# Attention scores without a mask product, zeros written into the exponentials by GpSimd, and low parts moved from GpSimd to VectorE

## The chip, the cores and the metric

One core of a Trainium2 chip runs the whole program. The metric is the device time of one execution in microseconds (us); for the kernel before it is the median of three runs. TensorE is called PE below, VectorE DVE, ScalarE ACT, GpSimd POOL, and the queue that issues the transfers SP.

## The reference

Twelve heads in each of two batches go through causal attention over 448 positions, and two feed-forward layers follow on the 896 tokens.

```python
scores = (q @ k.T) / 8
scores = where(mask, -1e9, scores)          # mask: key later than query
scores = scores - max(scores)
attn = exp(scores); attn = attn / (sum(attn) + 1e-9)
x = attn @ v                                # heads side by side: 896 x 768
h = x @ w_in                                # 768 x 1024
solu = h * softmax(h)
ln = (solu - mean) / sqrt(var + 1e-6) * g_ln
y = ln @ w_out                              # 1024 x 768
out = relu(y @ w_in2) ** 2 @ w_out2         # 768 x 2048 x 768
```

## The kernel before

The matrix products run on numbers split in two: a high part (a cast to the format that PE multiplies fast) and a low part (what the cast left out), in three products, high by high, high by low and low by high. So every operand costs one cast on ACT and one subtraction on DVE or POOL. The weights come in eight-byte form and are first put together as fp32 on DVE, by one tensor_scalar and two scalar_tensor_tensor (L150, L151, L152: "wf").

**Attention** goes over 12 pairs of heads, i = 0 to 11, two heads on the two halves of the partitions. For a pair: `load_r` and `load_v` bring k, q and v; `H` casts k and q (ACT), `L` makes their low parts (the tile LO, L272). `S0a`, `S0b`, `S0c` are products of the high parts alone (tile mxp), and `mxa`, `mxb`, `mxc` take from them, on DVE, the largest unmasked score of each query (L298, with a mask tile MK added). `mT` turns these maxima into a row on PE, `row` copies it (ACT), and `rowd` sends it to one partition of the tile MR by DMA (L323). `Sa` and `Sb` are the scores of the two halves of a pair's work, transposed (keys on the partitions): three products of parts, then one of MR with a constant of minus ones (NEG1), which subtracts the maxima, and then a masking product (L353) of a table TR of 0 and -1e30 with a shifted identity ID. Half a covers the first block of 128 keys for all queries, and the fourth block for the last 64; half b covers the second and the third block. `ea1` and `eb1` are the exponentials (ACT, into one of the buffers PP), `Ua` and `Ub` multiply by v, and a column of ones beside v gives the sums. `EA`, `EB` copy the result out, `sums`, `recips`, `rcd`, `spread` send the sums through DVE and a DRAM tile and back to 64 partitions (tile bc) by three DMAs, `norm` multiplies on POOL (tile x, one buffer, L419), and `x_hi`, `x_lo` split it. Pair 0 gets its maxima into the scores in another way (L359).

**The first layer** (`h0` to `h6`, seven tiles of 128 tokens, six chunks c of W1) begins while the last pairs run, the second (`y0`, `y1`) follows, then the two products with 2048 columns. W1 is loaded (`lq`, `ld`), expanded (`wf`), cast (`wh`, ACT) and its low part is made (`wl`: chunks 1, 3 and 5 on POOL, the others on DVE). `fl` are products whose result nobody reads, at the start.

What sets the order of all this is a list written into the kernel, SEQ: each name is an operation and its number a pair, a chunk or a tile. Each engine runs its own part of the list in that order, and waits where an operand or a buffer isn't ready. The products mxp, mT and U share four PSUM banks.

Of the kernel before, what the change touches and what calls it, by code (L numbers as in the profile page):

```python
# [29 lines left out]
load_r.2 fl.7 mxb.0 fl.8 lq.5 L.1 fl.9 S0c.1 fl.10 mxc.1 mxr.0 fl.11 S0a.1 S0b.1 Sa.0 mxb.1 H.2 load_r.3 lq.0 mxa.1  # L30
lq.6 L.2 mT.1 S0a.2 row.1 Sb.0 ea1.0 mxa.2 load_r.4 rowd.1 S0b.2 eb1.0 Ua.0 mxb.2 lq.1 lq.8 H.3 S0c.2 L.3 Ub.0 mxc.2
load_r.5 mT.2 Sa.1 row.2 EA.0 rowd.2 EB.0 load_v.2 S0a.3 ea1.1 S0b.3 sums.0 mxa.3 Sb.1 lq.9 lq.2 mxb.3 S0c.3 Sa.2 H.4
mxc.3 eb1.1 L.4 S0c.4 mT.3 ea1.2 mxc.4 Sb.2 recips.0 row.3 lq.3 S0b.4 eb1.2 rcd.0 Ua.1 mxb.4 load_v.3 rowd.3 S0a.4
Ub.1 mxa.4 spread.0 wf.0 load_r.6 Ua.2 lq.7 EA.1 H.5 mT.4 Sa.3 row.4 EB.1 norm.0 sums.1 S0b.5 load_v.4 ea1.3 Ub.2
mxb.5 rowd.4 L.5 load_r.7 x_hi.0 recips.1 Sb.3 EA.2 rcd.1 EB.2 S0c.5 sums.2 S0a.5 H.6 mxc.5 Sa.4 mxa.5 eb1.3 L.6 S0a.6
spread.1 mT.5 Sb.4 recips.2 lq.10 row.5 mxa.6 ea1.4 rcd.2 rowd.5 S0b.6 x_lo.0 H.7 Ua.3 mxb.6 load_r.8 norm.1 S0c.6
Ub.3 mxc.6 L.7 x_hi.1 spread.2 S0b.7 Sa.5 eb1.4 mxb.7 EA.3 EB.3 S0c.7 mT.6 mxc.7 Sb.5 wh.0 sums.3 x_lo.1 row.6 wl.0
ea1.5 S0a.7 rowd.6 Ua.4 H.8 load_v.5 norm.2 recips.3 load_r.9 mxa.7 eb1.5 rcd.3 Ub.4 lq.11 wf.1 mT.7 EA.4 Sa.6
load_v.6 EB.4 row.7 sums.4 S0c.8 ea1.6 Sb.6 spread.3 rowd.7 L.8 mxc.8 S0b.8 H.9 Ua.5 mxb.8 load_v.7 x_hi.2 eb1.6
x_lo.2 Ub.5 recips.4 wh.1 norm.3 rcd.4 load_r.10 S0a.8 Sa.7 mxa.8 L.9 EA.5 spread.4 x_hi.3 mT.8 S0a.9 EB.5 Sb.7 mxa.9  # L40
row.8 sums.5 ea1.7 load_r.11 x_lo.3 S0c.9 Ua.6 H.10 rowd.8 mxc.9 norm.4 eb1.7 load_v.8 recips.5 S0b.9 rcd.5 Ub.6 mxb.9
ld.5 wl.1 x_hi.4 mT.9 EA.6 Sa.8 row.9 EB.6 x_lo.4 sums.6 S0a.10 ea1.8 Sb.8 spread.5 L.10 mxa.10 load_v.9 rowd.9 S0b.10
H.11 Ua.7 mxb.10 ld.3 norm.5 S0c.10 Ub.7 mxc.10 recips.6 rcd.6 wf.2 mT.10 EA.7 Sa.9 row.10 eb1.8 S0b.11 EB.7 Sb.9
x_hi.5 spread.6 ea1.9 sums.7 L.11 mxb.11 Ua.8 load_v.10 rowd.10 x_lo.5 S0a.11 Ub.8 mxa.11 norm.6 recips.7 rcd.7 S0c.11
Sa.10 mxc.11 ld.4 wf.3 EA.8 eb1.9 mT.11 Ua.9 row.11 ea1.10 rowd.11 Sb.10 x_hi.6 spread.7 wh.3 Ub.9 wh.2 eb1.10 wl.2
Sa.11 EB.8 x_lo.6 sums.8 load_v.11 Sb.11 norm.7 ea1.11 h0.0 recips.8 wf.4 rcd.8 EA.9 Ua.10 eb1.11 x_hi.7 EB.9 h0.1
spread.8 sums.9 x_lo.7 wh.4 h1.0 wl.3 Ua.11 recips.9 norm.8 rcd.9 Ub.10 wf.5 h1.1 x_hi.8 spread.9 h0.2 h1.2 wl.4 wh.5
h0.3 EA.10 x_lo.8 EB.10 wl.5 h1.3 sums.10 h0.4 norm.9 recips.10 Ub.11 rcd.10 h1.4 EA.11 x_hi.9 spread.10 EB.11 x_lo.9
h0.5 sums.11 h1.5 mx.0 h2.0 norm.10 ex.0 recips.11 mx.1 rcd.11 load_g.0 h2.1 mu.0 x_hi.10 h2.2 spread.11 x_lo.10 sq.0
de.0 h2.3 ex.1 va.0 pw.0 h2.4 mu.1 norm.11 h2.5 h3.0 mx.2 x_hi.11 h3.1 fa.0 de.1 ln.0 x_lo.11 h3.2 lw.0 ex.2 h3.3 sq.1  # L50
de.2 mu.2 h4.0 va.1 sq.2 h3.4 va.2 lw.1 of.0 T.0 pw.2 pw.1 h3.5 Th.0 h4.1 fa.2 mx.3 h4.2 fa.1 ex.3 Tl.0 lw.2 h4.3 ln.2
of.1 h5.0 oh.0 ln.1 h4.4 ol.0 de.3 h4.5 mu.3 lw.3 h5.1 of.2 sq.3 T.1 oh.1 h5.2 Th.1 mx.4 h5.3 Tl.1 ex.4 lw.4 h5.4 va.3
ol.1 pw.3 h5.5 fa.3 mu.4 ln.3 h6.0 of.3 sq.4 T.2 lw.5 T.3 Th.2 mx.5 h6.1 Tl.2 ex.5 h6.2 oh.2 mu.5 h6.3 Th.3 de.4 h6.4
lw.6 oh.3 Tl.3 sq.5 h6.5 va.4 ol.2 pw.4 y0.0 mx.6 de.5 ex.6 ol.3 lw.7 fa.4 l2.2 y0.1 de.6 ln.4 mu.6 l2.1 l2.0 of.4
y0.2 va.5 oh.4 of.5 pw.5 y0.3 ol.4 fa.5 of.6 ln.5 y0.4 oh.5 sq.6 ol.5 va.6 of.7 T.4 pw.6 y0.5 Th.4 oh.6 Tl.4 oh.7 ol.6
T.5 fa.6 y0.6 Th.5 ln.6 Tl.5 ol.7 T.6 y0.7 Th.6 Tl.6 f2.0 y1.0 g2.0 yo.1 o2.0 y1.1 yp.0 yo.2 f2.1 y1.2 yp.1 g2.1 yo.0
o2.1 yp.2
# [3 lines left out]
def attention_moe_kernel(tc, kq, v, w_in, w_out, g_ln, w_in2, w_out2, out):  # L61
# [27 lines left out]
    def f(ap):  # L89
        return ap.bitcast(F32)  # L90

    with es:
# [84 lines left out]
        with att:  # L177
# [154 lines left out]
            def scores(n):  # L332
# [4 lines left out]
                for K, Q in ((HIk, HIq), (LOk, HIq), (HIk, LOq), (None, MR[i % 3])):  # L337
                    if K is None and i in mr:
                        continue
                    for t, o, q0, nq in HALF[a]:  # L340
                        M = D if K is None and t == 3 else P
                        for h in range(2):
                            r = slice(D * h, D * h + D)
                            k = NEG1[r, 0:M] if K is None else K[r, P * t : P * t + M]
                            nc.tensor.matmul(s[:M, h, o : o + nq], k, Q[r, q0 : q0 + nq], start=first, stop=False)  # L345
# [515 lines left out]
```

## Time and profile before

| | |
|---|---|
| median of three runs | 469.99 us (469.32 to 470.15) |
| the profiled execution, its own time | 469.13 us |
| its span, first to last instruction | 467.3 us |
| PE busy | 458.8 us (98%) |
| DVE, ACT, POOL busy | 267.4, 165.8, 134.4 us |
| granted clock of PE | 1.00 in every stretch |

The time of the profiled execution is 1.8 us longer than its span, since it holds what lies around the first and the last instruction. An engine counts as busy while one of its instructions runs; what it does not show is whether another engine would have let it start earlier. The first layer's products begin at 101.65 us; before that the core is in attention.

### The profile page before, as it was taken

How to read it: one execution, taken by the hardware profiler on the slowest of the kernel's cores; microseconds unless marked ns; L12 is line 12 of the kernel's file. 1: busy time of each engine (PE TensorE's matmuls, PEld its weight loads, DVE VectorE, ACT ScalarE, POOL GpSimd, SP SyncE). 2: the span in 40 equal slices, each digit the busy share in tenths (PEclk: the TensorE clock that was granted, in tenths of full speed). 3: DMA queues.
4: the chain of work that ended last, by engine and by line, in shares of the span. 5: the costliest groups of instructions: out<-in, count | busy, mean ns of one | idle time of the engine just before them, and what ended most of it. 6: DMA issues, size and time to landing. Idle time of an engine off the chain costs nothing.

```text
span 467.3 us, 6795 instructions
## 1 busy us (share of the span) xinstructions
PE 458.8 (98%) x2659; PEld 410.0 (88%) x2659; DVE 267.4 (57%) x514; ACT 165.8 (35%) x225; POOL 134.4 (29%) x95
## 2 busy tenths in 40 slices
...
GB/s 265 152 157 139 114 165 219 123 125 39 23 103 320 0 182 157 2 0 1 0 69 135 74 130 106 97 135 74 129 104 100 136 74 131 199 122 135 79 59 118
DMA packets 41713, 52.48 MB, mean 112 GB/s; under 512 B 18257, under 2 KB 32337, under 8 KB 41297
## 3 DMA queue, kind: packets, MB, share of 16 engines
...
## 4 chain that ended last, share of the span: by engine, by line
PE 92%; DVE 5%; issue 1%; DMA 1%; POOL 1%; ACT 1%; SPq 0%; DVEq 0%; ACTq 0%; POOLq 0%
PE h L775 25%; PE o L804 25%; PE y L641 12%; PE h L494 12%; PE U L377 8%; PE s L345 4%; DVE JK L298 2%; PE mxp L283 2%; PE T L619 1%; DMA bc<-d 1%; PE s L353 1%; DVE wf L151 1%; POOL x L419 1%; PE fill L523 1%; PE mT L306 0%
## 5 line engine op out<-in xcount | busy, mean ns | idle before, releaser
L697 POOL TENSOR_TENSOR w<-wf,w 128x768 fp32r<-128x768 f32 x32 | 59.2, 1851 | 207.4 <-ACT w L694 207.4
L775 PE MATMUL h<-yT,w 128*128 128x448 f32 x576 | 116.9, 365 | 0.0
L804 PE MATMUL o<-w,g 128*128 128x384 f32 x672 | 116.7, 336 | 0.0
L804 PEld LDWEIGHTS o<-w,g 128*128 128x128 f32 x672 | 116.5, 188 | 0.0
L775 PEld LDWEIGHTS h<-yT,w 128*128 128x128 f32 x576 | 108.2, 188 | 8.6
L694 ACT CAST w<-wf 128x768 fp32r<-128x768 f32 x32 | 26.8, 837 | 140.9 <-DVE wf L152 95.7
L150 DVE TENSOR_SCALAR wf<-raw 128x768 int32<-128x768 int32 (+1 forms) x46 | 27.7, 602 | 82.8 <-DMA raw<-in_moe_w_out_dram 57.4
L494 PE MATMUL h<-w,xT 128*128 128x512 f32 x252 | 59.2, 393 | 0.0
L641 PE MATMUL y<-lnT,w 128*128 128x384 f32 (+1 forms) x288 | 58.9, 365 | 0.0
L641 PEld LDWEIGHTS y<-lnT,w 128*128 128x128 f32 x288 | 51.9, 188 | 5.9
L494 PEld LDWEIGHTS h<-w,xT 128*128 128x128 f32 x252 | 46.9, 188 | 9.6
L298 DVE CUSTOM_DVE_ANT_0 JK<-mxp,MK 112x336 bf16<-112x336 f32 (+2 forms) x96 | 40.0, 446 | 24.8 <-PE mxp L283 21.3
L151 DVE SCALAR_TENSOR_TENSOR wf<-raw,wf 128x768 int32<-128x768 int32 (+1 forms) x46 | 51.2, 1112 | 1.6
L377 PE MATMUL U<-PP,VR 128*128 128x448 f32 (+1 forms) x192 | 48.6, 399 | 0.8 <-DVE mx L298 0.7
L152 DVE SCALAR_TENSOR_TENSOR wf<-raw,wf 128x768 int32<-128x768 int32 (+1 forms) x46 | 48.3, 1049 | 1.6
L377 PEld LDWEIGHTS U<-PP,VR 128*128 128x128 f32 x192 | 32.0, 190 | 16.1 <-issue 9.6
L419 POOL TENSOR_TENSOR x<-E,bc 64x448 f32<-64x448 f32 x24 | 30.5, 1270 | 40.8 <-DVE xT L431 23.3
L272 POOL TENSOR_TENSOR LO<-r,HI 128x896 fp32r<-128x896 f32 x12 | 26.9, 2245 | 14.6 <-ACT HI L268 14.2
L368 ACT ACTIVATE PP<-s 128x1024 f32<-128x1024 f32 x24 | 24.4, 1018 | 7.2 <-PE s L353 5.3
L761 DVE TENSOR_TENSOR relu<-h,relu 128x896 f32<-128x896 f32 x16 | 17.5, 1092 | 14.6 <-ACT relu L760 14.6
L389 ACT ACTIVATE E<-U,SE 128x448 f32<-128x448 f32 x24 | 14.6, 630 | 24.1 <-POOL x L419 15.1
L763 ACT CAST g<-relu 128x896 fp32r<-128x896 f32 x16 | 15.1, 941 | 18.6 <-DVE relu L761 18.6
...
## 6 DMA issues: line engine op xcount, KB each, us to landing
...
```

The costliest lines, as they stand in the source:

```text
L150: nc.vector.tensor_scalar(xi, hw, 3, 0x3FFFFFFF, ALU.logical_shift_left, ALU.bitwise_and)
L151: nc.vector.scalar_tensor_tensor(xi, hw, -0x40000000, xi, ALU.bitwise_and, ALU.bitwise_or)
L152: nc.vector.scalar_tensor_tensor(xi, lw, 29, xi, ALU.logical_shift_right, ALU.bitwise_or)
L272: eng.tensor_tensor(LO[i % 3][:, :, 0:S], kq_raw.pop(i), f(HI[i % 3][:, :, 0:S]), ALU.subtract)
L298: nc.vector.tensor_tensor_reduce(JK[t], bs[h][0:JP, o : o + nk], MK[:, S - nk :], 1.0, NEG, ALU.add, ALU.max, mx[i][:, 4 * h + t : 4 * h + ...
L377: nc.tensor.matmul(UB[i][h][:, q0:S], VR[i % 3][:, t, h, :], PP[(2 * i + a) % NPP][:, h, o : o + nq], start=t == 0, stop=t == 2,)
L419: nc.gpsimd.tensor_tensor(x[D * h : D * h + D], e[0:D, h], bc[:, h], ALU.mult)
L494: nc.tensor.matmul(b[:, half, :], xT[c][s][:, t * P : t * P + P], W1[c][:, w, 512 * half : 512 * half + 512], start=(c == 0 and s == 0 and ...
L641: nc.tensor.matmul(b[:, ci, 0:n], WO[fi][:, w, c * P : c * P + P], M["lnT"][a][s][:, fi, :], start=(fi == 0 and w == 0 and s == 0), stop=( ...
L697: nc.gpsimd.tensor_tensor(W2[n][:, 1], w_f["2", n], f(W2[n][:, 0]), ALU.subtract)
L775: nc.tensor.matmul(b[:, a, 0:HT], W2[fi][:, w, c * P : c * P + P], yT[c][s][:, HT * a : HT * a + HT], start=(c == 0 and w == 0 and s == 0) ...
L804: nc.tensor.matmul(ob, G[fi + e][s][:, P * t : P * t + P], w, start=(fi + e == 0 and r == 0), stop=(fi + e == NF2 - 1 and r == 2),)
```

## The change

The table TR, the identity ID and the masking product of both halves go, with their preparation on POOL and DVE at the start. Behind each exponential a new operation, `ka` or `kb` (function `causal`), writes zeros over the masked part of the two diagonal blocks, in place in PP, by two `affine_select` on POOL: one of 2x64 and one of 2x128 columns in half a, two of 2x128 in half b. PP gets a fifth buffer. The tile MR becomes 64 columns wider and holds the maxima of the last 64 queries ahead of all of them, so that half a subtracts its maxima with one product of 512 columns a head in place of one of 448 and one of 64; `rowd` issues two more small DMAs for a pair. The low parts of k and q of pairs 1 to 11 and of W1's chunks 1, 3 and 5 move from POOL to DVE. SEQ is a new list throughout. Two of the twelve `fl` go.

```diff
-LO_POOL = (1, 3, 5,)
-KLO_POOL = (0, 1, 2, 3, 4, 5, 6, 7, 8, 9, 10, 11)
-NPP = 4
+LO_POOL = ()
+KLO_POOL = (0,)
+NPP = 5
...
-load_r.0 load_v.0 fl.0 fl.1 fl.2 H.0 load_r.1 fl.3 lq.4 load_v.1 L.0 S0c.0 S0a.0 fl.4 mxa.0 fl.5 mxc.0 fl.6 S0b.0 H.1
+load_r.0 lq.0 fl.0 fl.1 fl.2 H.0 load_r.1 fl.3 lq.8 lq.1 L.0 S0b.0 fl.4 mxb.0 fl.5 S0a.0 fl.6 mxa.0 S0c.0 H.1 load_r.2
...
-            MR = [qk.tile([P, S], F32R, name=f"MR{i}") for i in range(3)]
+            MR = [qk.tile([P, D + S], F32R, name=f"MR{i}") for i in range(3)]
...
-            nc.gpsimd.memset(f(TR), 0.0)
-            for j in range(2):
-                for o, n in ((0, D), (D, P), (D + P, P)):
...
-                for h in range(2):
-                    nc.vector.tensor_copy(ID[D * h : D * h + D, j], ident[D * j : D * j + D])
-            nc.vector.tensor_copy(TR[D:P], f(TR[0:D]))
...
-                        f(MR[i % 3][D * h : D * h + 1]).rearrange("o (t p) -> o t p", p=JP),
+                        f(MR[i % 3][D * h : D * h + 1, D:]).rearrange("o (t p) -> o t p", p=JP),
                         f(m2[4 * h : 4 * h + 4]),
                     )
+                    nc.sync.dma_start(f(MR[i % 3][D * h : D * h + 1, 0:D]), f(m2[4 * h + 3 : 4 * h + 4, JP - D :]))
...
-                for K, Q in ((HIk, HIq), (LOk, HIq), (HIk, LOq), (None, MR[i % 3])):
+                for K, Q in ((HIk, HIq), (LOk, HIq), (HIk, LOq)):
...
-                for j in range(2):
+                for o, x, n in () if i in mr else (((0, 0, D + S),), ((192, D + P, S - P), (0, D + 2 * P, S - 2 * P)))[a]:
                     for h in range(2):
                         r = slice(D * h, D * h + D)
-                        b = s[:, h, 0 : 192 * a + 192].rearrange("p (a c) -> p a c", c=192)[:, :, 0 : 192 - 64 * a]
-                        x = TR[r, j, 64 * a : 192 + 128 * a].rearrange("p (a c) -> p a c", a=1 + a)
-                        nc.tensor.matmul(b, ID[r, j], x, start=False, stop=j == 1 and i not in mr)
+                        nc.tensor.matmul(
+                            s[:, h, o : o + n], NEG1[r], MR[i % 3][r, x : x + n], start=False, stop=o == 0
+                        )
...
+            def causal(n):
+
+                p = PP[n % NPP]
+                for o, m in ((0, D), (D, P)) if n % 2 == 0 else ((0, P), (192, P)):
+                    ap = p[:, :, o : o + m]
+                    nc.gpsimd.affine_select(ap, ap, [[0, 2], [1, m]], ALU.is_ge, 0.0, base=0, channel_multiplier=-1)
```

On PE, at the end of half a of pair 1, the kernel before runs these rows (s are the scores, mxp the products for the maxima; HI and LO are the parts of k and q):

```order
L345 MATMUL s<-LO_128,HI_125 128x448 x2
L345 MATMUL s<-LO_128,HI_125 128x64 x2
L345 MATMUL s<-MR_131,NEG_133 128x448 x2
L345 MATMUL s<-MR_131,NEG_133 64x64 x2
L353 MATMUL s<-TR,ID 128x192 x4
L283 MATMUL mxp<-HI_124 128x448 x2
```

The changed kernel runs these at the same place:

```order
L329 MATMUL s<-LO_128,HI_125 128x448 x2
L329 MATMUL s<-LO_128,HI_125 128x64 x2
L337 MATMUL s<-MR_131,NEG_133 128x512 x2
L270 MATMUL mxp<-HI_124 128x448 x2
L329 MATMUL s<-HI_125 128x320 x2
```

The four masking products are gone, and two products of 512 columns stand for four of 448 and 64; what followed moves up.

On POOL, in the middle of attention, the queue of the kernel before alternates between low parts (LO) and the normalisation (x):

```order
L272 TENSOR_TENSOR LO_129<-r,HI_126 128x2x448
L272 TENSOR_TENSOR LO_127<-r,HI_124 128x2x448
L419 TENSOR_TENSOR x<-E,bc 64x448 x2
L272 TENSOR_TENSOR LO_128<-r,HI_125 128x2x448
L419 TENSOR_TENSOR x<-E,bc 64x448 x2
```

In the changed kernel it alternates between selects on the exponentials (PP, of pairs 2 and 3) and the normalisation of pairs 0 and 1:

```order
L358 AFFINE_SELECT PP_143<-PP_143 128x2x128 x2
L358 AFFINE_SELECT PP_147<-PP_147 128x2x64
L358 AFFINE_SELECT PP_147<-PP_147 128x2x128
L412 TENSOR_TENSOR x<-E,bc 64x448 x2
L358 AFFINE_SELECT PP_144<-PP_144 128x2x64
L358 AFFINE_SELECT PP_144<-PP_144 128x2x128
L358 AFFINE_SELECT PP_145<-PP_145 128x2x128 x2
L412 TENSOR_TENSOR x<-E,bc 64x448 x2
```

The low parts have left this queue, and selects that PE's products U wait for stand in it behind a normalisation.

On DVE, between the third and the second group of maxima of pair 4 (JK is where the maxima's by-product goes), the kernel before has only the reciprocals of pair 0:

```order
L298 ISA JK_137,mx<-mxp,MK 112x224
L298 ISA mx 112x1
L400 RECIPROCAL sr<-sc 112x8
L298 ISA JK_138,mx<-mxp,MK 112x336
L298 ISA mx 112x1
```

The changed kernel makes the low parts of pair 4 there first:

```order
L285 ISA JK_137,mx<-mxp,MK 112x224
L285 ISA mx 112x1
L259 TENSOR_TENSOR LO_128<-r,HI_125 128x2x448
L393 RECIPROCAL sr<-sc 112x8
L285 ISA JK_138,mx<-mxp,MK 112x336
L285 ISA mx 112x1
```

One subtraction of 128x896 has come into DVE's queue between two groups of maxima.

## Rows read from the trace of the kernel before

**Rows 1.** Chain that ended last, from the page: share of the span by engine.

```profile
PE 92%; DVE 5%; issue 1%; DMA 1%; POOL 1%; ACT 1%; SPq 0%; DVEq 0%; ACTq 0%; POOLq 0%
```

**Rows 2.** Busy time of each engine in two stretches (start:end length, then us busy and instructions).

```profile
core 0: us, PE busy (x) PEld busy (x) DVE busy (x) ACT busy (x) POOL busy (x), PEclk, DMA share, GB/s
0.00:101.70 101.70, 96.54 (x784) 74.95 (x784) 71.27 (x245) 53.42 (x77) 52.70 (x46) 1.00 0.56 165
101.70:467.30 365.60, 362.30 (x1878) 335.08 (x1876) 196.16 (x270) 112.41 (x148) 81.69 (x50) 1.00 0.31 98
```

**Rows 3.** Waits of PE, whole span: us in total, times, longest us.

```profile
PE mT L306 <- DVE mx L298: 1.0, 3, 0.5
PE U L377 <- DVE mx L298: 0.7, 1, 0.7
PE mxp L283 <- DVE mx L298: 0.6, 2, 0.4
PE s L345 <- ACT PP L368: 0.6, 1, 0.6
```

**Rows 4.** PE in order of time: start us, us, line, operation, out<-in, count.

```profile
59.43 0.47 PE L345 MATMUL s<-MR,NEG 64*128 64x448 f32 x4
59.74 0.45 PE L353 MATMUL s<-TR,ID 64*128 64x192 f32 x4
60.02 0.29 PE L283 MATMUL mxp<-HI 64*128 64x224 f32 x2
...
61.16 0.42 PE L353 MATMUL s<-TR,ID 64*128 64x256 f32 x4
61.42 0.37 PE L283 MATMUL mxp<-HI 64*128 64x336 f32 x4
...
76.59 0.39 PE L283 MATMUL mxp<-HI 64*128 64x448 f32 x2
76.82 0.40 PE L345 MATMUL s<-HI 64*128 64x320 f32 x4
```

**Rows 5.** DVE in order of time, before the first maxima.

```profile
3.85 0.87 DVE L254 CAST ID<-ident 64x128 fp32r<-64x128 f32 x4
...
5.37 1.57 DVE L257 MEMSET VR<- 128x512 f32 x3 [0.15 <-issue]
...
6.86 0.56 DVE L298 CUSTOM_DVE_ANT_0 JK<-mxp,MK 112x448 bf16<-112x448 f32 x1
```

**Rows 6.** Groups by shape: line, count | busy us, mean ns | idle before, its releasers.

```profile
L766 DVE TENSOR_TENSOR g<-relu,g 128x896 fp32r<-128x896 f32 x16 | 17.4, 1085 | 1.0 <-ACT g L763 1.0
...
L419 POOL TENSOR_TENSOR x<-E,bc 64x448 f32<-64x448 f32 x24 | 30.5, 1270 | 40.8 <-DVE xT L431 23.3 <-DMA bc<-d 13.4 <-DVE mx L298 3.3
L272 POOL TENSOR_TENSOR LO<-r,HI 128x896 fp32r<-128x896 f32 x12 | 26.9, 2245 | 14.6 <-ACT HI L268 14.2
...
L250 POOL TENSOR_SCALAR_AFFINE_SELECT TR<-TR 64x64 fp32r<-64x64 f32 x2 | 0.6, 285 | 0.1
...
masks.py:199 POOL TENSOR_SCALAR_AFFINE_SELECT ident<-ident 128x128 f32<-128x128 f32 x1 | 0.3, 294 | 0.0
```

**Rows 7.** DVE and POOL in order of time, around two expansions of W1.

```profile
83.69 2.97 POOL L272 TENSOR_TENSOR LO<-r,HI 128x896 fp32r<-128x896 f32 x1
...
84.73 3.01 DVE L152 SCALAR_TENSOR_TENSOR wf<-raw,wf 128x1024 int32<-128x1024 int32 x1
...
94.70 1.22 DVE L152 SCALAR_TENSOR_TENSOR wf<-raw,wf 128x1024 int32<-128x1024 int32 x1
```

**Rows 8.** Order of time: SP's row of maxima, its use on PE; SP's sums, their use.

```profile
38.56 1.28 SPq L323 DMA_DIRECT2D MR<-m  x2
...
42.72 0.48 PE L345 MATMUL s<-MR,NEG 64*128 64x448 f32 x4
...
99.42 0.58 SPq L394 DMA_DIRECT2D sc<-E  x1
...
101.48 0.20 DVE L400 RECIPROCAL sr<-sc 112x8 f32<-112x8 f32 x1 [1.74 <-DMA sc<-E]
```

More of the change, by code (lines that the diff above doesn't have):

```diff
@@ L16 @@
 NEG = -3.0e38
-HUGE = -1.0e30
 UB_ = 3
@@ L28 @@
 SEQ = """
-load_r.0 load_v.0 fl.0 fl.1 fl.2 H.0 load_r.1 fl.3 lq.4 load_v.1 L.0 S0c.0 S0a.0 fl.4 mxa.0 fl.5 mxc.0 fl.6 S0b.0 H.1
[L30 to L57, printed above, removed]
+load_r.0 lq.0 fl.0 fl.1 fl.2 H.0 load_r.1 fl.3 lq.8 lq.1 L.0 S0b.0 fl.4 mxb.0 fl.5 S0a.0 fl.6 mxa.0 S0c.0 H.1 load_r.2
+fl.7 lq.4 fl.8 mxc.0 load_v.0 S0c.1 fl.9 mxc.1 S0a.1 mxr.0 lq.2 mxa.1 S0b.1 Sa.0 mxb.1 H.2 load_r.3 mT.1 S0a.2 row.1
@@ new lines @@
+Sb.0 ea1.0 mxa.2 load_v.1 ka.0 lq.3 lq.5 S0b.2 eb1.0 rowd.1 Ua.0 mxb.2 lq.9 H.3 kb.0 L.1 S0c.2 Ub.0 mxc.2 load_r.4 L.2
+mT.2 Sa.1 row.2 L.3 EA.0 rowd.2 EB.0 S0a.3 ea1.1 Sb.1 lq.6 mxa.3 sums.0 lq.10 S0c.3 ka.1 eb1.1 mxc.3 load_r.5 S0b.3
+load_v.2 mxb.3 Sa.2 H.4 kb.1 S0c.4 mT.3 mxc.4 Sb.2 row.3 L.4 rowd.3 S0b.4 Ua.1 recips.0 mxb.4 rcd.0 H.5 load_r.6 ea1.2
+wf.0 Ub.1 eb1.2 spread.0 load_v.3 S0a.4 EA.1 Sa.3 EB.1 kb.2 mxa.4 sums.1 S0c.5 Sb.3 ka.2 mxc.5 mT.4 norm.0 S0b.5 row.4
+wh.0 mxb.5 Ua.2 rowd.4 ea1.3 recips.1 rcd.1 x_hi.0 ka.3 S0a.5 load_v.4 H.6 Ub.2 mxa.5 eb1.3 wl.0 S0a.6 spread.1 EA.2
@@ new lines @@
+Sa.4 load_r.7 EB.2 kb.3 mxa.6 sums.2 mT.5 Sb.4 row.5 x_lo.0 ea1.4 rowd.5 L.5 S0b.6 Ua.3 norm.1 mxb.6 H.7 recips.2
+S0c.6 Ub.3 rcd.2 mxc.6 ka.4 eb1.4 load_r.8 x_hi.1 L.6 S0a.7 EA.3 Sa.5 EB.3 kb.4 mxa.7 spread.2 lq.7 mT.6 Sb.5 row.6
+L.7 sums.3 ea1.5 rowd.6 S0c.7 x_lo.1 Ua.4 H.8 load_v.5 ka.5 mxc.7 eb1.5 norm.2 S0b.7 recips.3 Ub.4 mxb.7 rcd.3
+load_v.6 L.8 S0c.8 load_r.9 EA.4 Sa.6 EB.4 kb.5 mxc.8 spread.3 Sb.6 wf.1 lq.11 sums.4 mT.7 Ua.5 row.7 x_hi.2 rowd.7
+ea1.6 H.9 load_r.10 S0b.8 x_lo.2 Ub.5 mxb.8 eb1.6 norm.3 wh.1 recips.4 S0a.8 rcd.4 mxa.8 Sa.7 load_v.7 ka.6 EA.5 EB.5
@@ new lines @@
+S0c.9 kb.6 mT.8 mxc.9 Sb.7 sums.5 row.8 x_hi.3 spread.4 wl.1 ea1.7 S0a.9 rowd.8 Ua.6 eb1.7 mxa.9 load_r.11 ka.7 H.10
+x_lo.3 S0b.9 recips.5 Ub.6 norm.4 mxb.9 rcd.5 S0a.10 Sa.8 mxa.10 kb.7 EA.6 spread.5 x_hi.4 mT.9 L.9 S0c.10 EB.6 Sb.8
+row.9 sums.6 ea1.8 x_lo.4 Ua.7 rowd.9 mxc.10 H.11 L.10 load_v.8 eb1.8 ld.3 norm.5 S0b.10 recips.6 Ub.7 rcd.6 mxb.10
+S0b.11 kb.8 x_hi.5 Sa.9 mxb.11 EA.7 ka.8 EB.7 mT.10 Sb.9 wf.2 sums.7 row.10 ea1.9 rowd.10 S0a.11 Ua.8 eb1.9 spread.6
+load_v.9 ka.9 mxa.11 wh.2 Sa.10 recips.7 x_lo.5 rcd.7 S0c.11 Sb.10 mxc.11 norm.6 mT.11 load_v.10 Ub.8 row.11 ea1.10
@@ new lines @@
+rowd.11 L.11 x_hi.6 spread.7 Ua.9 EA.8 x_lo.6 eb1.10 kb.9 EB.8 ka.10 Sa.11 sums.8 load_g.0 kb.10 Ub.9 ld.4 norm.7
+recips.8 Sb.11 wf.3 Ua.10 EA.9 ea1.11 EB.9 x_hi.7 h0.0 sums.9 eb1.11 load_v.11 wl.2 rcd.8 h0.1 wh.3 kb.11 h1.0 wf.4
+spread.8 Ub.10 ld.5 h0.2 wl.3 wh.4 h1.1 recips.9 ka.11 rcd.9 x_lo.7 Ua.11 norm.8 Ub.11 wf.5 EA.10 x_hi.8 h1.2 EB.10
+sums.10 h0.3 spread.9 wl.4 wh.5 h1.3 x_lo.8 wl.5 h0.4 norm.9 recips.10 h0.5 rcd.10 h1.4 mx.0 EA.11 h1.5 spread.10
+EB.11 ex.0 sums.11 h2.0 x_hi.9 x_lo.9 h2.1 de.0 norm.10 recips.11 mx.1 rcd.11 h2.2 mu.0 h2.3 x_hi.10 spread.11 sq.0
@@ new lines @@
+x_lo.10 h3.0 ex.1 va.0 pw.0 h2.4 mu.1 norm.11 h2.5 sq.1 h3.1 mx.2 x_hi.11 h3.2 de.1 ex.2 x_lo.11 va.1 lw.0 h3.3 pw.1
+mu.2 h3.4 fa.1 fa.0 de.2 ln.0 h3.5 sq.2 T.0 mx.3 lw.1 h4.0 va.2 ex.3 of.0 pw.2 h4.1 ln.1 h4.2 Th.0 fa.2 mu.3 oh.0 h4.3
+ln.2 lw.2 ol.0 T.1 sq.3 of.1 h4.4 h4.5 de.3 oh.1 Tl.0 h5.0 Th.1 lw.3 mx.4 h5.1 va.3 ex.4 Tl.1 h6.0 pw.3 mu.4 T.2 l2.0
+h5.2 de.4 sq.4 fa.3 ol.1 lw.4 h5.3 ln.3 of.2 h5.4 Th.2 T.3 of.3 h5.5 h6.1 mx.5 lw.5 h6.2 Tl.2 ex.5 h6.3 Th.3 de.5 mu.5
+h6.4 oh.3 Tl.3 sq.5 h6.5 lw.6 va.4 oh.2 y0.0 mx.6 ol.2 ex.6 ol.3 y0.1 de.6 va.5 mu.6 lw.7 pw.5 l2.1 pw.4 l2.2 fa.4
```

21 lines of the change are left out of this document (8 added, 13 removed).

## The prediction

> **What bounds the kernel now.** I read the chain that ended last first: PE holds 92% of it and DVE 5% [rows 1]. So the time is PE's work, and the question of any edit is how much of it PE loses and whether another engine then makes PE wait. Next the busy times before and after the point at which the first layer starts: up to 101.7 us PE is busy for 96.5 us, DVE for 71.3, POOL for 52.7; behind it PE is busy for 362.3 of 365.6 us [rows 2]. The reader is to see there that the later part is PE work alone, which this change leaves as it is, and that in attention DVE had 30 us to spare and POOL 49. The list of PE's waits shows how well attention is filled: apart from the wait for the first constants they are 1.0, 0.7, 0.6 and 0.6 us, 2.9 us in all, and all but one end with a maximum on DVE [rows 3]. Any gain has to come out of the first 100 us.
>
> **What the change takes from PE.** In the order of time the masking product of half a starts 0.28 us before the next instruction (59.74 to 60.02), that of half b 0.26 us (61.16 to 61.42) [rows 4]. I go by the distance between starts and not by the durations of 0.45 and 0.42 us, since matmuls overlap. With 12 halves of each, 12 x 0.28 + 12 x 0.26 = 6.5 us go. The maxima of half a take 0.31 us before (59.43 to 59.74). A pair of 448-column products with nothing behind it takes 0.23 us (76.59 to 76.82) [rows 4], so a pair of 512 columns should take 0.23 x 512/448 = 0.26. That saves 0.05 us in each of 11 pairs (pair 0 has another way), 0.5 us; the bounds are nothing and, if the 64 extra columns were free, 0.08 x 11 = 0.9.
>
> **The start.** DVE builds ID and TR from 3.85 to 5.37 us and takes the first maxima only at 6.86, behind the constants of v [rows 5]. That preparation goes, 1.5 us; MR's constants grow by a seventh, three times 0.06 us by the rate of the same memsets, 0.2 us. DVE gates the start, since PE's later products need the banks that the maxima release, so I count 1.3 us; the bounds are nothing (a late transfer of k and q takes the place) and 1.5. The two `fl` less lie where PE waits for DVE anyway and count for nothing; if PE didn't wait there, they would be a gain.
>
> **What DVE gets.** Its trace has no LO subtraction, but another subtraction of the same shape, 128x896, at 1085 ns [rows 6]. Eleven are 11.9 us, less the 1.3 us of the start: 71.3 + 11.9 - 1.3 = 81.9 us up to the end of the last scores. W1's three low parts on DVE come mostly later, where DVE has room; they are some 1.2 us each by the same rate. PE reaches that point at 101.7 - 6.5 - 0.5 - 1.3 = 93.4 us. So DVE would be busy for 88% of it, after 70%. That still fits, but DVE no longer has the slack that hid its expansions of W1, and PE's rows `mT` and mxp wait in turn for each group of maxima.
>
> Here a rule of the Trainium skill can be put beside a row. One last step of an expansion took 3.01 us from 84.73, while a POOL low part ran from 83.69 for 2.97 us; the same step at 94.70, with no POOL instruction running, took 1.22 us [rows 7]. SBUF — State Buffer, section Who interferes with whom, says that a DVE instruction with two SBUF inputs and a GpSimd instruction that reads SBUF lock each other out for a whole instruction, whichever comes second. The trace agrees (3.01 against 1.22 us). What the rule speaks of counts against this change: every moved subtraction has two such inputs, and POOL now runs 48 short selects among them. By the row a subtraction could lose 1.8 us; but the POOL instruction that cost it so much was of the kind that leaves POOL, so I take the locking as unchanged in sum and make the other case a rival.
>
> **What POOL gets and loses.** It loses 11 x 2.245 = 24.7 us of low parts [rows 6] and three of W1. It gets 48 selects. The trace has selects only of 64 and 128 columns and one plane, 285 and 294 ns; a low part's rate (2245 ns for 896 columns with two inputs) gives 0.64 us for 256 columns [rows 6]. I take 0.4 us, nearer to the selects, as they are the same operation: 48 x 0.4 = 19 us, with bounds of 14 and 31. POOL is no fuller than before. What is new is that U waits for it: exponential, two selects, product, so some 0.8 us later. The fifth PP buffer and the list give that time: behind `kb.2` and `ka.2` PE still has mxp and Sb rows before Ua.2.
>
> **What the transfers get.** `rowd` is now four issues instead of two. Two took 1.28 us [rows 8], so the row of maxima arrives 1.3 us later. Pair 4 shows the slack: the issue at 38.56, its second half 0.64 later, and then the landing, which for another small transfer was 2.06 us from issue to use (99.42 to 101.48), make 41.3; the product with MR started at 42.72 [rows 8]. So 1.4 us were spare, and 1.3 are taken. Where the list leaves little between `mT` and the scores (pair 2) I expect PE to wait 0.7 us; elsewhere a pair's U lies between. Bounds: nothing, and 1 us in a quarter of the pairs, 3 us.
>
> **The sum.** Gains 6.5 + 0.5 + 1.3 = 8.3 us. The 2.9 us of waits before are replaced by others: 0.7 for a late row of maxima and about 3.2 us for a DVE that is busy 88% and still does expansions of which one step can take 3.01 us [rows 7], my estimate, 3.9 in all, 1.0 more than now. Net 7.3 us: 469.13 - 7.3 = 461.8. The profiled execution lies 0.9 us below the median of the three runs, so the forecast for the median is 462.6 us.
>
> **The rivals.**
> *No wait left.* The new list could hide even what PE waits for now: 469.99 - 8.3 - 2.9 = 458.8. For it: DVE's load is even over the pairs; against it: less slack on DVE and SP. I give it to 460.
>
> *DVE sets the pace.* If each of the 11 subtractions is held by POOL for 1.5 us, nearly the 1.8 us of [rows 7], DVE's 81.9 us become 98.4, over PE's 93.4, and attention ends 5 us later than planned: a gain of 3.3 us at most, 466.7, and with the handshakes between PE and DVE up to 470. It decides from (93.4 - 81.9)/11 = 1.0 us a subtraction. Against it: the long POOL instructions are now only the 24 of `norm`. This is the case in which the rule of the Trainium skill on SBUF — State Buffer, Who interferes with whom, would rule the whole of attention.
>
> *POOL's queue holds U (slower).* POOL stood for 40.8 us in front of its 24 `norm` instructions, for x to come free or bc to land [rows 6]. That cost nothing while only low parts queued behind. If all of it stays and selects queue behind it, POOL's queue is 5 us of start + 2.2 for pair 0 + 40.8 + 30.5 [rows 6] + 48 selects. It passes 101.7 us from 0.48 us a select on; at the bound of 0.64 it is 109 us, and the time 469.99 + 7 = 477; halfway 473. Against it: part of that wait is POOL arriving early, 4 of the 24 lie behind attention, and the list puts the selects of pair 3 behind `norm.0` but a pair's scores and products ahead of Ua.3.
>
> **How the numbers follow.** Likeliest, PE stays the bound with 3 to 6 us of waits: 0.62, 460.5 to 465. No wait left 0.10. DVE sets the pace 0.18, three quarters of it still below the time before. POOL holds U 0.10. A difference under 0.2% (0.9 us) is about what three runs can't tell from none. Faster: 0.62 + 0.10 + 0.14 = 0.86; within 0.2%: 0.04; slower 0.10. The range for 8 in 10 goes from 459.5 to 467.5: it leaves out half of the best case, a fifth of DVE's case, and all of POOL's.
>
> **What would show it.** In the profile after: no masking product on PE, and scores of half a and b that follow in 1.2 and 1.0 us; selects of 0.3 to 0.6 us; low parts on DVE of 1.0 to 1.2 us, more where a `norm` runs; first maxima before 5.8 us; the first layer starting near 94 us, and PE's waits, fewer than 5 us, naming DVE's maxima. The later stages should keep their lengths. I would be wrong if the list of PE's waits named POOL's selects in front of U, if DVE were busy for over 95% of attention, or if PE stood in front of the first layer's last chunk, whose load now comes late in SP's queue.

## The result, and the profile after

Four executions of the changed kernel took 464.18, 464.80, 475.35 and 475.71 us, beside 469.65 us (469.09 to 470.15) for four of the kernel before on the same chip. The two long ones, and one of six of narrow_product below, ran at the full granted clock and left no profile, so their cause is open; the two others give a ratio to before of 0.989 (95% interval 0.9865 to 0.9915). The same kernel, run again later, took 464.69 us (464.13 to 465.05) in all four executions, beside 469.28 us: 0.990 (0.9886 to 0.9913). So the change gains about 4.6 us, where I had forecast 7.3.

The profiled execution took 464.80 us with a span of 463.1, after 469.13 and 467.3. Its chain that ended last, by engine, from the page:

```profile
PE 86%; DVE 2%; POOL 1%; ACT 1%; issue 1%; DMA 1%; SPq 1%; ACTq 0%; DVEq 0%; POOLq 0%
```

PE is still the bound; the chain now also passes through SP's queue (SPq), POOL and a DMA, which the account below comes back to. The same two stretches as in [rows 2], cut at the end of the last product of scores, which came at 101.65 us before and comes at 96.39 now:

```profile
core 0: us, PE busy (x) PEld busy (x) DVE busy (x) ACT busy (x) POOL busy (x), PEclk, DMA share, GB/s
0.00:96.39 96.39, 92.06 (x662) 68.24 (x662) 72.94 (x248) 51.41 (x75) 42.02 (x71) 1.00 0.56 152
96.39:463.10 366.71, 362.63 (x1878) 335.12 (x1876) 200.43 (x276) 114.24 (x150) 79.60 (x52) 1.00 0.32 103
```

Two things stand in it. Attention is 5.3 us shorter, and the part behind it 1.1 us longer (366.71 after 365.60). And DVE, which took over 11 low parts, is busy for 72.94 us of the first stretch, after 71.27: hardly more than before, where I had counted on 81.9. All of PE's waits in the whole span (us in total, times, longest):

```profile
PE fill L517 <- DVE NEG L232: 2.2, 1, 2.2
PE s L329 <- ACT PP L361: 0.6, 1, 0.6
PE h L488 <- ACT PP L361: 0.6, 1, 0.6
PE mxp L270 <- DVE mx L285: 0.4, 2, 0.2
PE mT L293 <- DVE mx L285: 0.4, 1, 0.4
PE mT L293 <- ACT E L382: 0.2, 1, 0.2
PE mxp L270 <- ACT E L382: 0.2, 1, 0.2
```

Apart from the first, for constants, these are 2.4 us, after 2.9 in [rows 3]. No wait in this list is one of U, and none ends with POOL. The names have changed, though: before, maxima on DVE ended nearly all waits; now 1.6 of the 2.4 us end with ACT (the exponentials into PP, the copy E).

**Where the time went.** To see this I add up, over all rows of PE in order of time from the first `mT` of a pair (mT.1) to the last product of scores, the distance from each row's start to the next row's start, and put it to the row's operation; a wait then counts with the row before it. Rows of the kind that this sum rests on, from PE in order of time after (start, us):

```profile
14.26 0.26 PE L293 MATMUL mT<-ident,mx 112*8 112x112 f32 x1
...
73.59 0.48 PE L337 MATMUL s<-MR,NEG 64*128 64x512 f32 x2
74.00 0.26 PE L293 MATMUL mT<-ident,mx 112*8 112x112 f32 x1
...
86.46 0.47 PE L337 MATMUL s<-MR,NEG 64*128 64x512 f32 x2
86.77 0.27 PE L270 MATMUL mxp<-HI 64*128 64x224 f32 x2
...
96.39 2.16 PE L370 MATMUL U<-PP,VR 128*128 128x448 f32 x8
99.15 0.74 PE L488 MATMUL h<-w,xT 128*128 128x512 f32 x2 [0.60 <-ACT PP L361]
```

| from mT.1 to the last scores, us | before | after | difference |
|---|---|---|---|
| masking products | 6.86 | 0 | -6.86 |
| products that subtract the maxima | 6.31 | 7.58 | +1.27 |
| mxp | 11.26 | 11.79 | +0.53 |
| the other products of scores | 20.00 | 19.86 | -0.14 |
| U | 39.13 | 39.55 | +0.42 |
| mT | 2.00 | 2.10 | +0.10 |
| in all (with 1.25 for pair 0's own way in both) | 86.80 | 82.13 | -4.67 |

The masking products are worth what I had read from [rows 4]. The row of maxima is not: the pair of 512 columns took 0.31 us to the next row at 86.46, exactly what 448 and 64 columns took in [rows 4], and 0.41 in front of an `mT` (73.59). The 1.27 us in the table are not the price of the width. The run narrow_mr below has the new list and the narrow row; its pairs take 0.31 us in front of mxp and 0.41 in front of `mT` too, and all its products that subtract maxima 7.40 us:

```profile
71.84 0.48 PE L337 MATMUL s<-MR,NEG 64*128 64x448 f32 x4
72.25 0.26 PE L293 MATMUL mT<-ident,mx 112*8 112x112 f32 x1
```

What the 1.27 us are, the rows show in part. The last row of the scores takes some 0.1 us more in front of `mT`, U or h than in front of mxp. Before, that was a masking row (0.28 us in front of mxp, 0.38 and 0.49 in front of `mT`), and some 0.6 of the 6.86 us were of this kind; now it is the row of maxima. And the new list puts `mT` behind the scores seven times, the old one twice.

mT.1 itself begins at 14.26 us, after 14.85, so the start gave 0.59 in this profile. With the 4.67 that makes 5.26 us at the end of the last scores. Of these, 0.9 are given back where the first layer begins: the second layer's first product starts at 165.62 us, after 169.99, which is 4.4 us earlier. Behind that point nothing moves much; the span is 4.2 us shorter.

### The profile page after: what moved, and what is told of

Its sections match the earlier page's. It is cut to its first block, busy times and chain, and to the rows that moved or that the text cites. A ratio compares the mean times of both kernels' runs of the same rounds, so it can differ in the third digit from the quotient of the medians.

```text
span 463.1 us, 6653 instructions
## 1 busy us (share of the span) xinstructions
PE 454.7 (98%) x2537; PEld 403.4 (87%) x2537; DVE 273.4 (59%) x523; ACT 165.7 (36%) x225; POOL 121.6 (26%) x122
## 4 chain that ended last, share of the span: by engine, by line
PE 86%; DVE 2%; POOL 1%; ACT 1%; issue 1%; DMA 1%; SPq 1%; ACTq 0%; DVEq 0%; POOLq 0%
PE h L769 25%; PE o L798 25%; PE y L635 13%; PE h L488 12%; PE U L370 6%; PE s L329 2%; PE T L613 1%; PE mxp L270 1%; POOL x L412 1%; DMA bc<-d 1%; DVE JK L285 1%; PE s L337 1%; ACT E L382 0%; PE mT L293 0%; SPq L310 0%
## 5 line engine op out<-in xcount | busy, mean ns | idle before, releaser
L150 DVE TENSOR_SCALAR wf<-raw 128x768 int32<-128x768 int32 (+1 forms) x46 | 26.4, 574 | 88.0 <-DMA raw<-in_moe_w_out_dram 57.7
L488 PEld LDWEIGHTS h<-w,xT 128*128 128x128 f32 x252 | 46.8, 188 | 10.4 <-ACT PP L361 0.7
L151 DVE SCALAR_TENSOR_TENSOR wf<-raw,wf 128x768 int32<-128x768 int32 (+1 forms) x46 | 48.1, 1046 | 1.6
L152 DVE SCALAR_TENSOR_TENSOR wf<-raw,wf 128x768 int32<-128x768 int32 (+1 forms) x46 | 45.8, 995 | 1.6
L412 POOL TENSOR_TENSOR x<-E,bc 64x448 f32<-64x448 f32 x24 | 28.2, 1176 | 32.6 <-DMA bc<-d 19.2
L358 POOL TENSOR_SCALAR_AFFINE_SELECT PP<-PP 128x256 f32<-128x256 f32 (+1 forms) x48 | 25.3, 558 | 34.9 <-ACT PP L361 34.3
```

Source lines behind the costliest of these rows:

```text
L150: nc.vector.tensor_scalar(xi, hw, 3, 0x3FFFFFFF, ALU.logical_shift_left, ALU.bitwise_and)
L151: nc.vector.scalar_tensor_tensor(xi, hw, -0x40000000, xi, ALU.bitwise_and, ALU.bitwise_or)
L152: nc.vector.scalar_tensor_tensor(xi, lw, 29, xi, ALU.logical_shift_right, ALU.bitwise_or)
L412: nc.gpsimd.tensor_tensor(x[D * h : D * h + D], e[0:D, h], bc[:, h], ALU.mult)
L488: nc.tensor.matmul(b[:, half, :], xT[c][s][:, t * P : t * P + P], W1[c][:, w, 512 * half : 512 * half + 512], start=(c == 0 and s == 0 and ...
```

## The experiments

The times below are medians. My theory: the masking products that PE no longer runs are the gain, and the four DMAs of `rowd`, in SP's queue, take a part of it back. The rivals are that DVE's new load or the lock between DVE and POOL takes it, that U waits for POOL's selects, that the wide product is itself the cost, and that the new list alone makes the gain.

**again.** The changed kernel without an edit, so that it stands beside the others on one chip.

> The changed kernel once more, as the base for the others: 464 to 465 us (ratio to before 0.987 to 0.991).

464.69 us, as told above. This is the number that the edits of the changed kernel are compared with.

**before_no_mask.** The kernel before, with its own list and engines, without its masking products.

```diff
-                for j in range(2):
-                    for h in range(2):
...
-                        nc.tensor.matmul(b, ID[r, j], x, start=False, stop=j == 1 and i not in mr)
```

> The kernel before without the four masking products a half, nothing put in their place, so that masked keys are counted; order, low parts and maxima as before. Theory A (what PE loses with the masking products is the whole gain, and the rest of the change only makes it possible): 463 to 465 us, as the changed kernel or up to 1 us better. Theory B (the new order and the shift of work give part of the gain, the old order would turn PE's saving into waits for DVE's maxima): 466 to 468 us.

466.75 us (466.14 to 467.50), 0.9942 (0.9929 to 0.9956): 2.5 us of the 6.5 that the products took. The preparation of TR and ID at the start stays in this run. Its waits of PE:

```profile
PE mT L306 <- DVE mx L298: 2.0, 4, 0.7
PE U L374 <- DVE mx L298: 1.9, 2, 1.6
```

With two of 0.7 and 0.6 us for ACT, its waits are 5.2 us, where [rows 3] has 2.9. In the old list PE arrives earlier and then stands for maxima that DVE doesn't deliver any faster. So the removal alone does not bring its price; the list has to be made for it.

**no_select.** The changed kernel without the selects on POOL.

```diff
-                    nc.gpsimd.affine_select(ap, ap, [[0, 2], [1, m]], ALU.is_ge, 0.0, base=0, channel_multiplier=-1)
+                    pass
```

> The changed kernel without the selects on GpSimd, so that masked keys are counted; all else as it is. Theory A (GpSimd's queue has room and the product with v doesn't wait for it): within 0.7 us of the changed kernel. Theory B (selects hold back PE, or lock VectorE's two-input instructions out): 1.5 us or more below it, 463 us or less.

465.58 us (465.13 to 465.92), against 464.69: taking 26 us of work off POOL gains nothing. The selects hold nobody up. It is 0.9 us slower, just outside the 0.7 of the first theory and on the other side from the second. Why isn't settled; its profile has a wait of 0.8 us in a late stage (`o` for a DVE result) that the changed kernel's hasn't, but one profile doesn't show that this is the cause.

**narrow_mr.** The changed kernel with the row of maxima as before: one small DMA a head, one product of 448 and one of 64 columns in half a.

```diff
-                    nc.sync.dma_start(f(MR[i % 3][D * h : D * h + 1, 0:D]), f(m2[4 * h + 3 : 4 * h + 4, JP - D :]))
...
-                for o, x, n in () if i in mr else (((0, 0, D + S),), ((192, D + P, S - P), (0, D + 2 * P, S - 2 * P)))[a]:
+                for t, o, q0, nq in () if i in mr else HALF[a]:
...
-                            s[:, h, o : o + n], NEG1[r], MR[i % 3][r, x : x + n], start=False, stop=o == 0
+                            s[:M, h, o : o + nq], NEG1[r, 0:M], MR[i % 3][r, D + q0 : D + q0 + nq], start=False, stop=o == 0
```

> The changed kernel with the maxima of half a subtracted as before (448 and 64 columns a head) and rowd back to two DMAs a pair. Theory A (the wide row saves PE nothing, and its 22 added issues delay the loads and the spread of the sums behind them in SP's queue): 0.7 to 2 us less than the changed kernel, 462.5 to 464; PE's wait of 0.6 us in front of the first layer is gone. Theory B (the sum of the prediction: the wide row saves PE 0.5 us and costs a wait of 0.7): within 0.5 us of the changed kernel.

462.73 us (462.49 to 462.86), 0.9858 (0.9845 to 0.9872): 2.0 us faster than the changed kernel. The part of the change that I forecast to cost 0.2 us in all, a saving of 0.5 less a wait of 0.7, costs 2.0. Its waits of PE, without the first:

```profile
PE mT L293 <- DVE mx L285: 0.3, 1, 0.3
PE mxp L270 <- DVE mx L285: 0.2, 1, 0.2
PE h L488 <- ACT PP L361: 0.2, 1, 0.2
```

0.7 us are left of 2.4, and those that went are the ones that end with ACT. The profiles show the way from SP to ACT at two places. The first is the wait of 0.6 us of `s`, early in attention. SP's issue of the load of k and q of pair 5 and ACT's cast of it, in the changed kernel:

```profile
26.50 0.37 SPq L221 DMA_DIRECT2D r<-in_kq_dram  x1
31.73 0.94 ACT L255 CAST HI<-r 128x896 fp32r<-128x896 f32 x1 [4.13 <-PE U L370]
```

and in narrow_mr:

```profile
24.72 0.38 SPq L221 DMA_DIRECT2D r<-in_kq_dram  x1
30.10 0.94 ACT L255 CAST HI<-r 128x896 fp32r<-128x896 f32 x1 [2.84 <-DMA r<-in_kq_dram]
```

The cast begins 5.2 us behind the issue in the one and 5.4 in the other, so I take the load for what it waits for in both, though the first row names PE. Behind the cast in ACT's queue stand the exponentials of pair 2, for which `s` waits in the changed kernel at 33.64 us; in narrow_mr, with the load 1.8 us earlier, it doesn't. The wait of `s` is in the profiles of all runs of the new list with four DMAs (0.4 to 0.6 us) and of none with one or two.

The second place is in front of the first layer. First the chain that ended last, of the changed kernel (start, us, engine):

```profile
88.68 0.68 SPq L310
...
90.72 0.52 SPq L314
...
91.35 3.26 DMA bc<-d
...
95.96 1.57 POOL x L412
...
97.55 0.03 ACT E L382
```

The four issues of `rowd.11`, of which the first and the last stand here, take 2.6 us of SP, and the DMA that brings back the sums of pair 7 (bc, part of `spread`) stands behind them. `norm` on POOL waits for it; ACT's next copy into E, of which there are two buffers, waits until `norm` has read the older one; and behind E in ACT's queue stands an exponential for which the first layer's `h` waits 0.60 us. Now SP in order of time in narrow_mr, at the same place:

```profile
87.00 1.33 SPq L310 DMA_DIRECT2D MR<-m  x2
89.04 0.52 SPq L405 DMA_DIRECT2D bc<-d  x1
```

Two issues take 1.33 us, bc is issued at 89.04 in place of 91.35, and `h` starts at 97.04 us, after 99.15; its wait is 0.2 us. Much of these 2.1 us had been lost earlier: the last scores end at 94.71 us in narrow_mr, after 96.39. Against my forecast, the late row of maxima is not what PE waits for; what stands behind it in SP's queue is.

**narrow_product.** The same without the first line of that edit: narrow products, but all four DMAs. It tells the product from the issues.

> The changed kernel with the maxima of half a subtracted by products of 448 and 64 columns, but with all four DMAs of rowd kept. Theory A (the cost of the wide row lies in SP's queue): 464 to 465.3 us, as the changed kernel (464.7), and PE again waits in front of the first layer. Theory B (the product of 512 columns is what costs): 462.5 to 463.2, as narrow_mr (462.7).

465.77 us in the median of six (464.57 to 475.38), 0.9914 (0.9901 to 0.9928): no better than the changed kernel, and 0.5 us over the range of the first theory. So the DMAs cost the 2.0 us, not the product. Its waits at the first layer are back:

```profile
PE h L489 <- DVE w L484: 0.8, 1, 0.8
PE h L489 <- ACT PP L362: 0.7, 1, 0.7
```

**wide_two_dmas and narrow_one_dma.** Both send the maxima of both heads in one DMA, to two partitions at a time. The first keeps the wide row with a second such DMA, the second has the narrow row.

```diff
-                for h in range(2):
-                    nc.sync.dma_start(
-                        f(MR[i % 3][D * h : D * h + 1, D:]).rearrange("o (t p) -> o t p", p=JP),
-                        f(m2[4 * h : 4 * h + 4]),
-                    )
-                    nc.sync.dma_start(f(MR[i % 3][D * h : D * h + 1, 0:D]), f(m2[4 * h + 3 : 4 * h + 4, JP - D :]))
+                nc.sync.dma_start(f(MR[i % 3][0:P:D, D:]).rearrange("o (t p) -> o t p", p=JP), f(m2[0:8]))
+                nc.sync.dma_start(f(MR[i % 3][0:P:D, 0:D]), f(m2[3:8:4, JP - D :]))
```

> The changed kernel with its wide row of maxima, sent with two DMAs a pair instead of four: one for both heads' 448 columns, one for both heads' 64. Theory A (the number of issues in SP's queue is the cost of the wide row): 462.4 to 463.3 us, as narrow_mr (462.7). Theory B (the width itself costs, in the product or in the landing): 464 to 465.3, as the changed kernel (464.7).

> narrow_mr with one DMA a pair for both heads. Theory A: PE has 0.7 us of waits left in narrow_mr, so at most that much less: 462.0 to 462.8 us. Theory B (SP's queue still holds back the kernel): 461.5 or less.

wide_two_dmas: 463.17 us (461.71 to 464.40), 0.9866 (0.9850 to 0.9883). narrow_one_dma: 462.38 us (461.66 to 462.74), 0.9849 (0.9836 to 0.9861), with the lowest median of all. By DMAs per pair the times are 464.69 (four), 463.17 and 462.73 (two, wide and narrow), 462.38 (one). The second pair of DMAs costs 1.5 to 2.0 us, and the second DMA another 0.35, within the spread of the runs. The idle time between PE's rows from mT.1 to the first `h`, added up from starts and lengths, goes the same way: 2.58 us in the changed kernel's profile and 2.10 in again, 2.20 in narrow_product, 0.99 in both wide_two_dmas and narrow_mr, 0.84 in narrow_one_dma. With equal numbers of DMAs the wide row isn't shown to gain or to lose.

**low_on_gpsimd.** The changed kernel, with the low parts back on POOL.

```diff
-LO_POOL = ()
-KLO_POOL = (0,)
+LO_POOL = (1, 3, 5,)
+KLO_POOL = (0, 1, 2, 3, 4, 5, 6, 7, 8, 9, 10, 11)
```

> The changed kernel with the low parts of k, q and three chunks of W1 back on GpSimd, 32 us more in the queue in which the selects stand. Theory A (GpSimd's queue is in order, so low parts and selects hold each other up and PE waits for scores and for U; the move to VectorE is what makes room): 467 us or more. Theory B (GpSimd has room for both and the move costs more on VectorE than it gives): 464 us or less.

468.45 us (467.46 to 469.30), 0.9977 (0.9967 to 0.9987): 3.8 us slower than the changed kernel, as the theory had it that counts the move as needed. Its first waits of PE:

```profile
PE U L370 <- DMA VR<-in_v_dram: 1.2, 1, 1.2
PE h L488 <- POOL w L483: 1.0, 1, 1.0
PE U L370 <- POOL PP L358: 0.7, 1, 0.7
```

Here U does wait for POOL's selects (0.7), and the first layer for a low part of W1 made on POOL (1.0). The move clears POOL's queue for the selects. Why v's transfer lands late here (1.2) is not shown.

**before_low_on_vector.** The kernel before, with the low parts on DVE, and nothing else; the edit above with its signs turned.

> The kernel before, masking products and old order kept, with the low parts of pairs 1 to 11 and of W1 on VectorE. Theory A (the move is covered only in an order that is made for it; in the old one each subtraction stands in front of maxima that PE waits for): 471 us or more, with PE waiting over 5 us for VectorE. Theory B (the move is free, as GpSimd locks VectorE out less): within 1 us of before.

468.82 us (468.33 to 471.08), 0.9991 (0.9980 to 1.0003). My theory had DVE's load make it slower, 471 us or more, and it fell; its rival, that the load is given back by less locking, held. The forms on DVE show how (count | busy us, mean ns | idle):

```profile
L272 DVE TENSOR_TENSOR LO<-r,HI 128x896 fp32r<-128x896 f32 x11 | 11.9, 1086 | 0.1
L151 DVE SCALAR_TENSOR_TENSOR wf<-raw,wf 128x1024 int32<-128x1024 int32 x6 | 8.2, 1361 | 0.2
L152 DVE SCALAR_TENSOR_TENSOR wf<-raw,wf 128x1024 int32<-128x1024 int32 x6 | 7.3, 1225 | 0.2
```

In the kernel before, the same view has:

```profile
L151 DVE SCALAR_TENSOR_TENSOR wf<-raw,wf 128x1024 int32<-128x1024 int32 x6 | 12.8, 2136 | 0.2
L152 DVE SCALAR_TENSOR_TENSOR wf<-raw,wf 128x1024 int32<-128x1024 int32 x6 | 9.9, 1658 | 0.2
```

The subtractions take 1086 ns, as the nearest row had said, and the expansions of W1 fell from 2136 and 1658 ns to 1361 and 1225 in the mean.

**no_mask_low_on_vector.** before_no_mask and before_low_on_vector in one.

> before_no_mask with the low parts on VectorE as well: the masking products are left out with nothing in their place, so that masked keys are counted; old order. Theory A (low parts on GpSimd lock VectorE's expansions out, which costs more than the moved subtractions add): 465 to 466.5 us, a little below before_no_mask (466.75). Theory B (without the masking products the old order runs at VectorE's pace, and 12 us more of it show): 468 us or more.

466.51 us in the median of twelve (466.24 to 472.71), 0.9963 (0.9937 to 0.9988). By its median it is where before_no_mask is (466.75): neither the loss of the second theory nor, clear of the spread, the small gain of the first. In the old list the move of the low parts opens nothing.

**old_order.** All of the change, but with the list of the kernel before, each select right behind its exponential.

```diff
-mT.2 Sa.1 row.2 L.3 EA.0 rowd.2 EB.0 S0a.3 ea1.1 Sb.1 lq.6 mxa.3 sums.0 lq.10 S0c.3 ka.1 eb1.1 mxc.3 load_r.5 S0b.3
...
+load_r.5 mT.2 Sa.1 row.2 EA.0 rowd.2 EB.0 load_v.2 S0a.3 ea1.1 ka.1 S0b.3 sums.0 mxa.3 Sb.1 lq.9 lq.2 mxb.3 S0c.3 Sa.2 H.4
```

> All of the change but the list: the old order, with each pair of selects put right behind its exponential. Theory A (PE's saving of some 6 us is eaten by waits for VectorE without the new list; in the old order without the masking product it was 2.5 us already): 468 us or more, no gain. Theory B (the parts give the gain and the order is minor): 466 us or less.

475.14 us (471.34 to 476.18), 1.0093 (1.0059 to 1.0126): slower than before, 10 us slower than the same parts in the new list, a part of it by a lower granted clock (0.993 to 0.996 over the execution), which the last section shows. Two of its waits of PE:

```profile
PE mxp L269 <- ACT E L381: 3.1, 1, 3.1
...
PE s L336 <- DMA MR<-m: 1.1, 1, 1.1
```

Here the row of maxima itself lands late (1.1 us), which the changed kernel's list avoids.

**old_order_narrow.** The same with the narrow row of narrow_mr.

> old_order with the narrow row and two DMAs a pair. Theory A (the added issues are what made the old order with all of the change lose 4 us against before): 463 to 467 us, faster than before. Theory B (the old order itself has no place for the selects): 470 us or more.

467.55 us in the median of ten (467.18 to 472.30), 0.9996 (0.9963 to 1.0029). One theory had 463 to 467, and even the fastest execution is just outside, so neither held cleanly. The profile (467.22 us) has waits of 1.9 us of U for POOL's selects and 2.0 of `mT` for maxima. Beside old_order the medians differ by 7.6 us, but not at the same clock: six of these ten executions ran at 0.999 or 1.000 (467.2 to 467.6 us), and four at 0.993 (471.7 to 472.3). Beside old_order's three at 0.993 (474.6 to 476.2) the narrow row is worth some 3.7 us in this list, beside 2.0 in the new one; the rest goes with the lower clock.

## Why the forecast was right in sign, and its gain 2.7 us too large

**What bounds the kernel, the likeliest case and the range** held: PE stays the bound, little but attention moves, and 464.7 us lies in 459.5 to 467.5. The forecast of 462.6 us (462.7 by its own terms) was 2.1 too low; the gain came out at 4.6 for 7.3.

**The masking products** (6.5 us): 6.86 measured. Reading them by the distance between starts was right; by their durations in [rows 4] they would have been 10.4 (24 times 0.42 to 0.45). Some 0.6 of the 6.86 did not go, as the table shows: it stands with the row of maxima now.

**The step that failed is the row of maxima**: "saves 0.05 us in each of 11 pairs", 0.5 us, and "I expect PE to wait 0.7 us" for four issues, a net loss of 0.2 us. The runs say a loss of 2.0 (464.69 less 462.73), inside the bounds that I gave (up to 3 lost), but by another mechanism. The saving isn't there (0.31 us before and after; I had taken a pair of mxp, 0.23 us, for the measure of it), and the cost isn't the row's own landing: PE never waits for MR in the changed kernel. I followed what is late next from `rowd` to the scores and not to the other issues in SP's queue, the sums and the loads of k, q and v, though four issues of some 0.6 us pass ahead of them in 11 pairs. narrow_product shows that the DMAs are it, wide_two_dmas that half of them suffice. That their place in SP's queue is the way, and not the transfers themselves, is read from the rows of SP and ACT and from the chain; no run separated the two.

**The start** (1.3 us): 0.6 measured. The bound that I named, another wait in place of the preparation, is what came. DVE in order of time after:

```profile
4.24 1.57 DVE L244 MEMSET VR<- 128x512 f32 x3
6.39 0.51 DVE L285 CUSTOM_DVE_ANT_0 JK<-mxp,MK 112x336 bf16<-112x336 f32 x1 [0.58 <-PE mxp L270]
```

DVE is free at 5.8 us, as forecast, and then waits 0.58 for PE's first product; the first maxima begin at 6.39, after 6.86 in [rows 5], and not before 5.8. That the 0.6 us come from the preparation isn't shown. With the old list and the low parts on DVE, mT.1 starts at 15.33 us with the preparation (before_low_on_vector) and at 15.14 and 14.91 without it (old_order, old_order_narrow), 0.2 to 0.4 earlier; in the other profiles of the new list with the low parts on DVE it starts between 13.41 and 14.43.

**What DVE gets** (81.9 us, 88% busy): 72.94 us and 76%. The low parts cost what I took (1123 ns against 1085), but "the locking as unchanged in sum" was wrong, on the good side. The forms on DVE after:

```profile
L259 DVE TENSOR_TENSOR LO<-r,HI 128x896 fp32r<-128x896 f32 x11 | 12.3, 1123 | 0.0
L151 DVE SCALAR_TENSOR_TENSOR wf<-raw,wf 128x1024 int32<-128x1024 int32 x6 | 8.2, 1374 | 0.2
L152 DVE SCALAR_TENSOR_TENSOR wf<-raw,wf 128x1024 int32<-128x1024 int32 x6 | 7.4, 1240 | 0.2
```

The twelve expansion steps lost 6 x (2136 + 1658 - 1374 - 1240) = 7.1 us against the kernel before, more than half of what the low parts brought. Before, six of the twelve took 1.22 to 1.23 us, three took 3.01 to 3.27 beside a low part on POOL, as in [rows 7], and three some 2.04 beside `norm`. After, nine take 1.22 to 1.23, one 2.04 beside `norm`, and two 1.31 beside selects. Not all of this lies in the stretch that I had forecast. Up to the end of the last scores, eight steps took 14.2 us before and six take 7.4 now: 4.4 us of the miss of 9.0 are what the eight had lost to POOL, and some 3.5 are that the new list has one expansion less there. The rival in which DVE sets the pace, at 1.0 us of hold for each subtraction, is out: they are held for some 0.04 us (1123 less 1085). The rule of the Trainium skill, SBUF — State Buffer, section Who interferes with whom, agrees with this trace: with the long POOL instructions gone, DVE's two-input steps run close to their own time (1374 and 1240 ns beside 1.22 us, and 1361 and 1225 in before_low_on_vector). What I had read as speaking against the change spoke for it: here a step lost 1.8 to 2.1 us beside a low part, 0.8 beside `norm` and 0.1 beside selects (a subtraction up to 0.2), and the long instructions were those that moved.

**The waits** (3.9 us, 3.2 of them behind DVE): 2.4 measured. I had them too long and put most of them to the wrong engine. That the forecast is no further off is luck: had I sized DVE rightly and SP's issues wrongly as I did, it would have been too low by still more.

**POOL and its queue.** The selects took 590 ns for 2x128 columns and 460 for 2x64, after the 0.4 us that I took, inside the bounds (0.285 to 0.64). Groups by shape on POOL after:

```profile
L412 POOL TENSOR_TENSOR x<-E,bc 64x448 f32<-64x448 f32 x24 | 28.2, 1176 | 32.6 <-DMA bc<-d 19.2 <-DVE mx L285 5.4 <-DVE LO L259 3.6
L358 POOL TENSOR_SCALAR_AFFINE_SELECT PP<-PP 128x256 f32<-128x256 f32 x36 | 20.6, 590 | 16.4 <-ACT PP L361 16.1
L358 POOL TENSOR_SCALAR_AFFINE_SELECT PP<-PP 128x128 f32<-128x128 f32 x12 | 5.5, 460 | 18.5 <-ACT PP L361 18.2
```

POOL still stands 32.6 us in front of `norm` and now 34.9 us in front of the selects, for the exponentials. So the selects are there before their data, and U waits for none of them; the slow rival, in which POOL's queue holds U, did not come. It is a matter of the list and of the moved low parts: U waits 1.9 us for POOL in old_order_narrow and 0.7 in low_on_gpsimd.

**No wait left** (460 us) was nearer than I thought for the change without its extra DMAs: narrow_one_dma has 0.5 us of waits of PE besides the first, and 462.38 us. What kept it from 460 isn't a 512-column product, which it hasn't: its mT.1 starts at 14.35 us, 0.5 earlier than before where I had counted 1.3, and its products that subtract the maxima take 7.36 us, 1.05 more than before where I had counted 0.5 less.

**Open** are the 0.9 us of no_select, the 1.2 us that U waits for v in low_on_gpsimd, what of the 0.6 us at the start is the preparation, and what the new list gains by itself: no run has it with the masking products kept.
